# Gated recurrence and long convolution on one core: transposing before the sigmoid, the product in PSUM, and a new order

## The chip, the cores and the metric

The kernel runs on one core of a Trainium2 chip. The core has a matrix engine (TensorE, PE in the profile, with PEld for its weight loads), VectorE (DVE), ScalarE (ACT), GpSimd (POOL) and SyncE (SP), which here only issues transfers. Every engine takes its own queue of instructions strictly in order; between engines semaphores hold an instruction until its inputs are there. Data lie in SBUF or in PSUM, 128 partitions each; PSUM has eight banks of 512 float32 a partition, TensorE writes there only, and GpSimd can't reach it. The metric is the device time of one execution in microseconds. Before the change it was 462.54 us, the median of two runs (459.77 and 465.32).

## The reference

Four batches of 6,272 steps of 256 channels, float32 in and out. A gated recurrence runs along time, and a gated long convolution takes its result:

```python
sig = 1 / (1 + exp(-f_logit))
f = lower_bound + (1 - lower_bound) * sig
h[t] = f[t] * h[t-1] + (1 - f[t]) * x[t]
proj = h @ w_proj                      # 256 -> 768: x1, x2, x3
X2 = rfft(x2, n=S); H = rfft(filter_fft, n=S)
y = x1 * irfft(X2 * H, n=S) * x3
out = y @ w_out
```

With s = sigmoid(-f_logit), 1 - f = (1 - lower_bound) s. The factor (1 - lower_bound) belongs to a channel, so the kernel takes it out of the recurrence and puts it into w_proj. What is left is u = s x and f = 1 - (1 - lower_bound) s, and the scan h[t] = f[t] h[t-1] + u[t].

## The kernel before

The transform of length 6272 = 128 x 49 is made of matrix products. `prepare` makes its tables and the spectrum of the filter (lines 425 to 689) and stores the spectrum in DRAM as H. Then, for each batch:

- `hgrn` (312 to 371), the recurrence, in 13 chunks of 512 steps (the last has 128). SyncE loads a chunk of f_logit into FL and of x into XT (three buffers each), 512 KB a load, with time on the partitions. Step "sig": ScalarE makes s in place in FL. Step "u": GpSimd multiplies x by s in place in XT. Step "su": for each half kh of the channels, TensorE transposes s and u into two PSUM banks (16 transposes of each at a time), so that channels come onto the partitions. Step "f": ScalarE, or for some chunks VectorE, makes f out of s in PSUM and writes it to fTs in SBUF. Step "scan": VectorE scans f from SBUF and u from PSUM into HA; a chunk's scan starts from the last column of the chunk before. "wrap" copies the first 3,072 columns behind the end of HA.
- `spectrum`: `phase_p` (696 to 711, "P") makes x2 from all of HA, 13 groups of four residues of 49, each copied to SBUF (X2) by ScalarE or VectorE ("x2"). Then 16 units: F1 and its copy "A", the mini product for one frequency with VectorE's "zm" (738 to 745, two instructions), F2, the product with the spectrum (794 to 811), I2 and its copy "Th". The spectrum product has two forms: VectorE multiplies out of PSUM ("MUL", line 798), or ScalarE or VectorE copies to SBUF and GpSimd multiplies there (line 807).
- `gate` (374 to 419): x1 and x3 from HA, and their product z; here too VectorE multiplies out of PSUM (line 408), or two copies are made and GpSimd multiplies (line 417).
- `phase_o` (838 to 882): the last step of the inverse transform, VectorE's product with z ("y", line 857), the projection "proj", a copy and the store.

The recurrence of the next batch overwrites HA, so its scans run among the gate's and the inverse's work of this batch, behind P.

No scheduler decides while the program is built. `Plan` records the steps, each with the engines that may take it, and `ORDER` (lines 123 to 190) is a string that lists all steps in the order of issue: for each its engine and its PSUM bank. It is a constant in the source; `emit` follows it, and the costs that the steps carry are not read for it. So each queue's order, the choice of engine for every copy, f and product, and the banks come from that string. A step that takes PSUM names the number of banks (`take`), and the steps with `src` read what it left there.

Of the kernel before, what the change touches and what calls it, by code (L numbers as in the profile page):

```python
# [34 lines left out]
WARM = 24  # L35
# [4 lines left out]
FS = 1.0 / 8.0  # L40
HS = 64.0 / S / FS
# [4 lines left out]
NX2 = 13  # L46
# [13 lines left out]
class Plan:  # L60
# [63 lines left out]
    "A0gA1AA5gA6AA+gBDgBIgBNgBSgAAYAOYABIACIAPIApQAdQAzYAqQAoQAkQAyQARIA2QA/YA4AA3AAQAAVYAXYBXgAhSAlSBhgBAQBJYBCAAUIA"  # L124
    "WIAfSBBIA7SBEAAvUBcgBFUBOYBGEBHEAiWBKWBTYBLGBrgBMGBPUBREBYYAnWASABmgA9CA8KBwgBZWBiIBUQBdYBbOBVIBQEBjSBsYBlCBaGAT"
    "IBeUBgEBfEBnIBtWEFgAYYBuGBkCBWIBoUBxIAZYAaYBqEByQBzAB0AAxSD5gBpMB3SB4KD7AB5QB6IB7YBvOB+UD6gCASCBKB8QB/EB9AD8YCJU"
    "ADgAEYCKMCHSCDQCICCEICCYEHACQUCLYD9SERgETAEGgEBWD+KD/KEIYCREECGEDOCOQCPACMUCNEESgEUYCTQAFgCUAEJSEKKELKCXUCSYCYEE"
    "NQEdgB1YB2YEegEOAEVUAHAEfAEPIEgYEWMEXMEZWCeSCfCEpgEYYCZQCgSEaGEbOCaACcQCdICbYEqgCnUChCCiYE1gE2gEhSElWFBgCoMErAEs"
    "YAKAEiCFCgEjKEkYEmGEnOCpQCqACwUCrYAIACjQCxME3AE4YCkAEtSAJAEuKEvKExWFLgCuUGHgEyGEzOCvECyYCsQFMgFDAFEYE5UE6ME7ME9S"
    "CtAE+CFVgE/KEwYC5WE8YC6GCzQC0AC+WFNAFFUFIQFWgFfgFggFGMC2gC/GFJIDASC3WFOYDBCFHMC4GC7YDCYFXAFYYDHSC8WFKIFPUFQMFSQF"  # L130
    "pgFqgFRMC9GDICDDWDJSFTAFUIFZUFaMDEGDKCDLYFbMDOWFhAFiYFcQFzgF0gDPGFdAFeIDQSDRCDSYDZWDMUDTSFjQDNMCGgFrAFsYAGgDaGDU"
    "CFkIFlICmgDeWDfGDXUDYEDbYF1AF2YALADgSDhKFmWF9gF+gFnOFoODcUDdEFtQFuAFvIDpSCFgFwUDnWDqCDjSFxEFyMAMAE0YDiYEEYEcYEoY"
    "DoGDrYF/AGAYF3QF4IDkCFAYDuWDvOANAMegF5IDwUDxEC1gF6SF7CF8KEAYDsWEMYJbUJcVJeNMqgDyYJgQJhRGBSDtGClgJdECVgEQYJfYJiAG"
    "CKDzWJjBJkYGDKDWgGEUD3QGIgJlSJmTGFMGGMD0GD2gGtgJnKJorGJUGKED4ADVgGPWGQOGbSGcCGdUGeMGLQGMAGRSGSKGVUGWMMgAGXQGYIGZ"
    "SGaCDFgGTWGUOCWgMsAGNUGOMGhQGiIDGgGfSGgCJqWJrXD1gJvUJxMJwQJyoJzYJsGJtHJuYGjSGkCJ0RGpUGqEJ1QJ2BJ3IJ4YGuSGwqGxYGlW"
# [12 lines left out]
    "MASMBKMFWMGOOcUOdEOeMOfQVLgVKgOgAOhIMCSMDCMEgMHWM1YOmUOnEOpSOqCOoMOrKVWgMKQMLIMPUMQMMIGMJgO6SO7KO8WO9GPCQPDAO4UO"
    "5EO+SO/KPEQVAAVXgPFAVBYO0WO1GOuUOvEOyQOzIOwSOxKVMAVNYOsUOtMVYAO2QO3IPAWPBGMMSMNCMUUMVMPKQPLIVZYPGWPHGMRSMOgMSCMZ"
    "UMaMR/YSEYPQWPUuPVYPIQPJAPMUPNEMTgPSuPTYSFSSHKSGTSIDSJYMWQPOUPPMPZYPRYMXAPYWPogPauPbYPcuPdYPpSPrCPgUPkESKQSMAPWR"  # L150
    "PhYPlYPisPjYPXBPzVP0FP7gSLQSPXSRHSNoPeRPqYPtqPuYPsYSQUSUQSWIPfBPxWPyGSVVSXtSYYSSESTYP3SP4KP1QP2APmWP8UPnGQAsQBYP"
    "vQP5SP6KQGYP9YPwAP+sP/YQFWQHGQEgQIYQJuQKYSZVQNgSbFQfQQgAQXSQOVSaUQSFSeQSgAScsSdYQbKMYgQWgQCWQPYQTYQDGQQtQRYSfRSj"
    "QShpSiYSkTSlAQpgSmDQhWQiGQLUQYYQcYSnYQZqQaYQMEQjQQkAQUWQVGSOYQqUQygQusQvYSoSSqCQlQQmAQssQtYSpTQ7gQdWQeGSrrSsYStS"
    "SvCQnQQoIQrYQ0YQzUREgQ3EQ4YQ1sQ2YRFWRJGRHGRNSROKQwQQ9YQxAQ8UQ+ERAsRBYQ/YRXgVCWVDGRPQRQAVEOVGSVjgVigRggQ5URGYRIYR"
    "KYVHCVIKQ6ERpgVOQRCWVPAVQIRDGRRURSESuSSyTS0DSwqSxYRYWSzQRauRbYS1oS2YS3RS5BRcuRdYS4SRTUS8TS+LS6CS7YS9QVSRVvgVugRU"
    "ERVURWMRZYRygRLWRiYS/ATAYVTBVUJTBQRMGVkAVlYRhURjsRkYRlsRmYVaWVbGTDAReSRrYVcORfCTCRTGUTIETHQRqSRuqRvYTEBTFYVeUV7g"
    "V6gVmWTJATKYVFgVfEVgMRsCRtYVnGTLQTNATMRTQSTRTTOpTPYVoOVqUWHgWGgVwATSCTTrTUYVrEVsMRnQR0YVxYVJgRoATVSTWWTaXTXCTcHT"
    "bQTYuTZYRzSR1qR2YR3qR4YTdATeYV8ARwURxEVyQV2WWRgWQgVzAV0IV3GV4OTfSTgUTkTTiETlVTpUThCTqQTmDTntToYV9YTjYTrMWIAV+SV/"
    "CWCWWagTuRR5UTwBTvRWAKTzSTsoTtYTxpTyYWJYWDGWEOT0TT4QV1YR6EWbgT1CT2DT3YMbUT5RMcET6AT9SWKUWNWWSAWTYMdgT7pT8YWBAWkg"
    "WOGUCQWLEV5YWcAWdYWlgT+KT/SUACUBgUDIUEQUFAVdYWMMUHUWPOWUSWmAUIMUMWUGgWVCUNOWXQWWKWugWYAWZIWvgUJUUKEUOWUPGURSUSKW"  # L160
    "eUWhQWFYVVYWfEWgMULgVpAWiAW4gW5gabWUQgacXaeHWnYadGUTSUUCUVgUWUWwAWxYUbWWjIVhYUXMWoQWpAagSahTaiCajDUYUUZEUcOUgWWq"
    "IUhOWrSWyQXDgXCgWsCUdUWtKW1WWzAW0IW6AW7YW2GW3OUeEUagUiSUjCUlQUqUUmIUrMXEAXFYUfgdfgW8WW9GW+OW/SXACXBKdqgUnQUsUUoA"
    "UpgdegXGWXHGXJQd3gUkgXIOU0SVtYVRYXKAXLIU1KUtEUvWXiQXjAdrgUwOd2gXaUXbEXSSXTKXeQXfAXcUXdEXWSXXKdgAdsAXkQXlAdhYXOWX"
    "POUugdtYXYUXZEXMSXNKXgQXhAXUUXVMXQSXRCUxQUyAUzgU5UU6MafYXoSakYXmWXnOXpCXqUXrMXsQXtAalSanCamTaorU2WU3GU4gXuQXvIX5"
    "YXwUXyEX0sX1YXzYYIgdiSdjCX4QapYX8oX9YYTWYUGXxYX6oYbgaqUarVdkKasEavRatFaxBYAWYEGYCOauYdmUeCgdnEdoMX2QYBYX7YX3AYFY"
    "awXdlgayvYDYYkga0Sa2Ca1TX+QYKYa3ra4YYRUYSMazYd4Ad5YduWdySX/AeOga5QdvGdwOdzCd0KYVUa7AYWEa6Ra+Qa8BYJWYNuYOYYLuYMYb"
    "AAYXUYYEYGSYHCa/QbDRbBobCYa9Yd6UbFBYZSYaKYdYd7Ed8MYtgYcWYeGYfYYguYhYYPQYmYYQAYuSbEWYyCeDgYwCbGGYlQZBUZCEYnoYoYY2"
    "gbHYd+Seagd/CYpoYqYYiWYvYYjGeAKYxYZJgbIQbKAePgYzYbJUdpYbNVbLsbPFYrWY4YYsOZSgY/QeEAY3SY5qeFYY7qY8YZbgZFUZAAebgZGE"
    "Y6YbOWbSXbUHbQGbRYbTQbVoZDRY0UY1MY9WZEBZHQZIIZUYZLYd9YecAZKSZMqZOqZNYZtUZPYZTQZXoZYYY+GZuEZVoZWYbXWbZGZkgbYXbaHb"
    "bYbcSbeCbWYbdUeGWZcSbfEbgYeHGeIObMYZQUZdYZgqZhYZeCZfYedYZvRZREbhQZ3gZxUZwBbjAZZWZmYeQAZaObiRbkpblYbmQboAZlSZyEeJ"  # L170
    "gZnqZoYbnWZpqZqYZiQaAgbpGbqYZjAeRYZzUZ4WZ8uZ9YZ0EbrSZ6uZ7YaJgbsQbwRbtCaSgbuAbvYZrUeKSbyBZ1QZ2IaCYZ5YZsEeLCeMKemg"
# [22 lines left out]
def kernel(  # L194
# [230 lines left out]
    def prepare(head, tmp):  # L425
# [522 lines left out]
```

## Time and profile before

| | us |
|---|---|
| device time, median of 2 runs | 462.54 |
| the two runs | 459.77, 465.32 |
| span of the profiled execution | 460.2 |
| sigmoid on ScalarE, line 324, 52 instructions | 53.0 |
| product u on GpSimd, line 326, 52 | 116.9 |
| f on ScalarE, line 351, 89 | 58.3 |
| f on VectorE, line 353, 15 | 10.2 |
| scans on VectorE, line 359, 104 | 122.0 |

The profile is of one execution, and its span is the only time of that execution that is shown. A group of instructions is one source line, engine, operation and shape: busy time, mean of one in ns, and how long the engine stood idle before them and for whom. Instructions of one engine overlap at their ends, so the busy times of groups add up to a little more than the engine's. The ends of matrix products are modelled in the profile.

### The profile page before, as it was taken

The numbers are of one execution on the slowest core, as the hardware profiler recorded it, in microseconds if no ns is written. First come the engines' busy times: TensorE is split into PE (matmuls) and PEld (weight loads), VectorE is DVE, ScalarE is ACT, GpSimd is POOL, SyncE is SP. The second block draws the span as 40 slices with busy tenths as digits, with TensorE's granted clock in tenths as the row PEclk, the third lists the DMA queues.
The fourth block names the chain that finished last, engine by engine and source line by source line (L and its number), as shares of the span: only waits on it lengthen the run. The fifth ranks groups of instructions, "written<-read, shape, count | busy, mean of one in ns | idle before, by whom it ended". The sixth has DMA issues, their size and how long they took to land.

```text
span 460.2 us, 14622 instructions
## 1 busy us (share of the span) xinstructions
PE 439.7 (96%) x6009; PEld 344.3 (75%) x6009; DVE 412.1 (90%) x471; ACT 402.7 (88%) x582; POOL 310.2 (67%) x293
## 2 busy tenths in 40 slices
PE   7799989999989999999999999999999999999997
PEld 5677778766756889778667889767768897777786
DVE  8689998899999996998999996999999987999872
ACT  6799988799999997899999988999998868989663
POOL 6889766188999643778898435789996603857400
PEclk9899999999999999999999999999999999999999
DMA  8967898986997997386887996579869830756176
GB/s 333 390 268 288 315 307 283 349 284 219 309 353 250 358 315 276 139 246 218 307 300 280 318 317 239 214 248 318 255 235 315 306 138 13 230 200 205 57 287 275
DMA packets 44242, 121.40 MB, mean 264 GB/s; under 512 B 4240, under 2 KB 6672, under 8 KB 44176
## 3 DMA queue, kind: packets, MB, share of 16 engines
q1 hardware_dynamic: 44176, 120.47, 74.0%
q8 instruction: 47, 0.77, 0.7%
q14 instruction: 19, 0.16, 0.1%
HBM read 87.69 MB, written 31.98 MB: 260 GB/s over the span
## 4 chain that ended last, share of the span: by engine, by line
PE 63%; DVE 12%; ACT 11%; DMA 5%; issue 5%; POOL 2%; SPq 0%; DVEq 0%; ACTq 0%; POOLq 0%
PE PS L387 14%; PE PS L817 8%; PE PS L869 7%; PE PS L338 7%; PE PS L705 6%; PE PS L777 6%; PE PS L718 5%; DVE HA L359 5%; PE PS L851 4%; DMA FL<-in_f_logit_dram 3%; DVE ys L857 2%; DVE X L286 2%; ACT FL L324 2%; PE PS L646 2%; ACT fTs L351 1%
## 5 line engine op out<-in xcount | busy, mean ns | idle before, releaser
L326 POOL TENSOR_TENSOR XT<-XT,FL 128x1024 f32<-128x1024 f32 (+1 forms) x52 | 116.9, 2251 | 50.3 <-ACT FL L324 41.9
L359 DVE TENSOR_TENSOR_SCAN HA<-fTs,HA,PS 128x512 f16<-128x512 f32 (+1 forms) x96 | 112.5, 1200 | 2.8 <-ACT fTs L351 1.7
L798 DVE TENSOR_TENSOR PP<-PS,Hu 98x1008 f16<-98x1008 f32 x87 | 101.3, 1197 | 3.4 <-ACT HA L281 1.4
L387 PE MATMUL PS<-HA,W 128*128 128x490 f16 (+1 forms) x416 | 100.4, 367 | 0.9 <-DVE X L286 0.4
L807 POOL TENSOR_TENSOR PP<-HA,Hu 98x1008 f16<-98x1008 f16 x41 | 86.2, 2107 | 1.7 <-PE PS L817 1.0
L281 ACT CAST HA<-PS 128x1024 f16<-128x1024 f32 (+1 forms) x94 | 77.0, 849 | 5.1 <-PE PS L718 3.4
L417 POOL TENSOR_TENSOR zt<-x1s,x3s 128x490 f16<-128x490 f32 (+1 forms) x43 | 52.3, 1222 | 41.8 <-ACT x3s L281 22.9
L857 DVE TENSOR_TENSOR ys<-PS,zt 128x1024 fp32r<-128x1024 f32 (+1 forms) x52 | 58.5, 1149 | 9.5 <-PE PS L851 5.0
L283 ACT ACTIVATE osb<-PS 128x1024 f32<-128x1024 f32 (+1 forms) x51 | 49.9, 992 | 13.9 <-PE PS L869 11.2
L351 ACT ACTIVATE fTs<-PS,nomc 128x512 f32<-128x512 f32 (+1 forms) x89 | 58.3, 679 | 3.7 <-PE PS L338 2.3
L387 PEld LDWEIGHTS <-W 128*128 128x128 f16 x416 | 35.4, 97 | 31.7 <-issue 5.4
L869 PE MATMUL PS<-Wo,ys 128*128 128x256 f32 x392 | 57.7, 292 | 1.3 <-DVE ys L857 1.1
L283 ACT ACTIVATE x1s<-PS 128x490 f32<-128x490 f32 (+1 forms) x92 | 53.5, 594 | 5.0 <-PE PS L387 3.0
L817 PEld LDWEIGHTS <-PP 98*128 98x128 f16 x1024 | 48.7, 98 | 10.6 <-issue 3.1
L324 ACT ACTIVATE FL<-FL 128x1024 f32<-128x1024 f32 (+1 forms) x52 | 53.0, 1026 | 2.2 <-DMA FL<-in_f_logit_dram 2.1
L869 PEld LDWEIGHTS PS<-Wo,ys 128*128 128x128 f32 x392 | 49.4, 188 | 5.8 <-DVE ys L857 2.2
L817 PE MATMUL PS<-VA,PP 98*128 98x98 f16 x512 | 52.2, 207 | 1.5 <-ACT x1s L283 0.8
L817 PE MATMUL PS<-VB,PP 98*128 98x98 f16 x512 | 51.9, 207 | 0.0
L281 ACT CAST Th<-PS 128x784 f16<-128x784 f32 x58 | 48.2, 830 | 2.6 <-PE PS L817 1.6
L338 PE MATMUL PS<-iden,FL 64*128 64x64 f32 x784 | 44.8, 230 | 1.6 <-DVE HA L359 0.9
L705 PE MATMUL PS<-W,HA 128*128 128x256 f16 x392 | 44.4, 273 | 1.0 <-ACT X L281 1.0
L705 PEld LDWEIGHTS <-HA 128*128 128x128 f16 x392 | 42.9, 142 | 1.9 <-issue 1.3
(113 smaller groups left out, 724.3 us busy)
## 6 DMA issues: line engine op xcount, KB each, us to landing
Hu<-H SPq DMA_DIRECT2D x55, 512.0 KB, 4.4
FL<-in_f_logit_dram SPq DMA_DIRECT2D x48, 512.0 KB, 5.4
XT<-in_x_dram SPq DMA_DIRECT2D x48, 512.0 KB, 5.5
out_dram<-osb SPq DMA_DIRECT2D x48, 512.0 KB, 4.3
X<-in_moe_filter_fft_dram SPq DMA_DIRECT2D x9, 512.0 KB, 7.1
H<-Hu SPq DMA_DIRECT2D x4, 512.0 KB, 6.2
Hu<-in_moe_filter_fft_dram SPq DMA_DIRECT2D x2, 512.0 KB, 9.8
H<-Hu SPq DMA_DIRECT2D x4, 256.0 KB, 6.5
```

Source lines behind the costliest of these rows:

```text
L281: nc.scalar.copy(dst, src)
L283: nc.scalar.activation(dst, src, AF.Copy, scale=scale)
L326: op("u", {"POOL": 0.1 + 0.553 * nb}, lambda e, xt=xt, ft=ft: nc.gpsimd.tensor_tensor(xt, xt, ft, op=AOP.mult), r=[("ft", k)], w=[("xt", k)])
L338: nc.tensor.transpose(bank(pb)[:, at[p] + j:at[p] + hn:nb], src[ps, j, cols], iden[ps, ps])
L359: nc.vector.tensor_tensor_scan(h, fT, bank(pb)[:, 512 - hn:512 + hn], init, op0=AOP.mult, op1=AOP.add),
L387: nc.tensor.matmul(PS[:, p, 0:n], W13[:, kh, js], HA[:, HB[kh] + t0:HB[kh] + t0 + n], start=(kh == 0), stop=(kh == 1))
L705: nc.tensor.matmul(pp[:, r - r0, :], column(HB[kh], q_of(r)), W2[:, kh, :], start=(kh == 0), stop=(kh == 1))
L798: nc.vector.tensor_tensor(pr, px.unsqueeze(1).broadcast_to([TB, 2, UE, 63]), hh, op=AOP.mult)
L807: nc.gpsimd.tensor_tensor(pr, spec[:, o, :, 1:64].unsqueeze(1).broadcast_to([TB, 2, UE, 63]), hh, op=AOP.mult)
L817: nc.tensor.matmul(PS[:, ib + o, pr * TB:(pr + 1) * TB], PP[:TB, k, o, n, 2 * pr:2 * pr + 2, :], v[:TB], start=(n == 0), stop=(n == 1))
L857: nc.vector.tensor_tensor(late["ys"][:, yk, :, 0:rn * 128], PS[:, cb:cb + 2, 0:rn * 128], late["zt"][:].rearrange("p k r m -> p k (r m)") ...
L869: nc.tensor.matmul(po[:, i, :], late["ys"][:, yk, kh, i * 128:(i + 1) * 128], Wo[:, kh, :], start=(kh == 0), stop=(kh == 1))
```

## The change

In `hgrn`, the transposes move ahead of the arithmetic:

- f_logit and x are transposed as they were loaded, each with a step "su" of its own that takes two PSUM banks for both halves of the channels (before, one step for each half held s and u of that half). The number of transposes is the same.
- The sigmoid reads f_logit out of PSUM and writes s, now with channels on the partitions, back into FL.
- f is made from s in SBUF by ScalarE or GpSimd; fTs has one place for each half.
- u is made by VectorE, a product of x in PSUM and s in SBUF, written in place into the middle of the two PSUM banks, where the scan reads it. The second half's product writes where the first half's scan has read, so it waits for that.

Around it: P has 12 groups, the last of five residues over three banks; zm is one instruction of 256 elements in place of two of 128; the warming products come in 48 steps of two in place of 24 of four; and `ORDER` is a new string, so the choices of engine change too (counts over the whole run):

| step | before | after |
|---|---|---|
| f | ScalarE 89, VectorE 15 | ScalarE 32, GpSimd 72 |
| u | GpSimd 52 (of 1,024) | VectorE 104 (of 512) |
| spectrum product | VectorE 87, GpSimd 41 | VectorE 71, GpSimd 57 |
| its copies | ScalarE 39, VectorE 2 | ScalarE 52, VectorE 5 |
| gate product | VectorE 61, GpSimd 43 | VectorE 52, GpSimd 52 |
| gate copies | ScalarE 131, VectorE 16 | ScalarE 138, VectorE 18 |
| wrap | GpSimd 34, ScalarE 8, SyncE 6 | GpSimd 24, ScalarE 5, SyncE 19 |

```diff
+            fl = ft.rearrange("p j d -> p (j d)")
+            def turn(pb, src, at, nb=nb, hn=hn):
+                for kh in range(2):
+                    for j in range(nb):
+                        for p in range(2):
+                            ps, o = slice(64 * p, 64 * p + 64), at[kh][p]
+                            nc.tensor.transpose(bank(pb)[:, o + j:o + hn:nb],
+                                                src[ps, j, kh * 128:kh * 128 + 128], iden[ps, ps])
+            tz = op("su", ..., turn(pb, ft, ((0, 512), (256, 768))), r=[("ft", k), "iden"], take=2)
+            def gate_s(e, pb, fl=fl, hn=hn):
+                z = PS[:, pb:pb + 2].rearrange("p a (k t) -> p k a t", k=2)[:, :, :, 0:hn]
+                nc.scalar.activation(fl.rearrange("p (k a t) -> p k a t", k=2, a=2), z,
+                                     AF.Sigmoid, scale=-1.0)
-            op("sig", ..., nc.scalar.activation(ft, ft, AF.Sigmoid, scale=-1.0), w=[("ft", k)])
-            op("u", {"POOL": ...}, nc.gpsimd.tensor_tensor(xt, xt, ft, op=AOP.mult))
+            op("sig", ..., gate_s, w=[("ft", k)], src=tz)
+            tx = op("su", ..., turn(pb, xt, ((512 - hn, 512), (0, 768))), r=[("xt", k), "iden"], take=2)
             for kh in range(2):
-                su = op("su", ..., turn, r=[("ft", k), ("xt", k), "iden"], w=["qT"], take=2)
+                fT, sT = fTs[:, kh, 0:n], fl[:, kh * n:kh * n + n]
                 def gate_f(...):
                     if e == "ACT":
                         nc.scalar.activation(fT, sT, AF.Identity, scale=by, bias=1.0)
                     else:
-                        nc.vector.tensor_scalar(fT, in0=sT, scalar1=by, scalar2=1.0,
+                        nc.gpsimd.tensor_scalar(fT, in0=sT, scalar1=by, scalar2=1.0,
                                                 op0=AOP.mult, op1=AOP.add)
+                def gate_u(e, pb, sT=sT, kh=kh, hn=hn):
+                    mid = bank(pb)[:, 512 - hn:512 + hn]
+                    xT = halves(pb, hn) if kh else mid.rearrange("p (a t) -> p a t", a=2)
+                    nc.vector.tensor_tensor(mid.rearrange("p (a t) -> p a t", a=2), xT,
+                                            sT.rearrange("p (a t) -> p a t", a=2), op=AOP.mult)
+                op("u", {"DVE": ...}, gate_u, r=[("ft", k)] + ([("hn", 0, c)] if kh else []),
+                   w=[("uT", tx, kh)], src=tx)
...
-            for e2 in range(2):
-                nc.vector.tensor_tensor(zp[:TB, q % 2, e2], ..., Hm[:TB, e2, :, :, es], op=AOP.mult)
+            nc.vector.tensor_tensor(zp[:TB, q % 2], px, Hm[:TB, :, :, :, es], op=AOP.mult)
```

More of the change, by code (lines that the diff above doesn't have):

```diff
@@ L250 @@
     dram = ctx.enter_context(tc.tile_pool(name="dram", bufs=1, space=bass.MemoryType.DRAM))
[L252 removed]
+    H = [dram.tile([2, M + HT, 2 * UE * 64], F16, name=f"H{u}") for u in range(NU // 2)]
     psp = ctx.enter_context(tc.tile_pool(name="psp", bufs=1, space=PSUM))
@@ L323, in hgrn @@
                    w=[t], dma=0.38 * nb, lag=2.4, margin=MARGIN)
-            op("sig", {"ACT": 0.095 + 0.213 * nb}, lambda e, ft=ft: nc.scalar.activation(
-                ft, ft, AF.Sigmoid, scale=-1.0), w=[("ft", k)], table="sigmoid")
-            op("u", {"POOL": 0.1 + 0.553 * nb}, lambda e, xt=xt, ft=ft: nc.gpsimd.tensor_tensor(
-                xt, xt, ft, op=AOP.mult), r=[("ft", k)], w=[("xt", k)])
-            for kh in range(2):
-                cols = slice(kh * 128, kh * 128 + 128)
-                hn = 64 * nb
-                def turn(e, pb, ft=ft, xt=xt, cols=cols, nb=nb, hn=hn):
-                    for src, at in ((ft, (0, 768)), (xt, (512 - hn, 512))):
-                        for j in range(nb):
-                            for p in range(2):
-                                ps = slice(64 * p, 64 * p + 64)
-                                nc.tensor.transpose(bank(pb)[:, at[p] + j:at[p] + hn:nb],
-                                                    src[ps, j, cols], iden[ps, ps])
-                su = op("su", {"PE": 0.126 * nb}, turn, r=[("ft", k), ("xt", k), "iden"], w=["qT"], take=2)
-                j = count["f"] % 2
-                count["f"] += 1
-                fT = fTs[:, j, 0:n]
```

209 lines of the change are left out of this document (108 added, 101 removed).

## The prediction

> **What bounds the kernel now.** I read the page's head and its chain of waits first, then the chain in order of time to find where each batch's projection P begins (line 705), then the busy times between those points.
>
> ```profile
> span 460.2 us, 14622 instructions
> PE 439.7 (96%) x6009; PEld 344.3 (75%) x6009; DVE 412.1 (90%) x471; ACT 402.7 (88%) x582; POOL 310.2 (67%) x293
> PE 63%; DVE 12%; ACT 11%; DMA 5%; issue 5%; POOL 2%; SPq 0%; DVEq 0%; ACTq 0%; POOLq 0%
> ```
> ```profile
> 75.70 5.25 PE PS L705 x48
> ...
> 172.74 1.91 PE PS L705 x16
> ...
> 273.02 3.66 PE PS L705 x32
> ...
> 371.44 6.27 PE PS L705 x56
> ```
> ```profile
> 0.00:75.70 75.70, 66.60 (x707) 50.82 (x708) 66.77 (x103) 66.26 (x99) 61.81 (x86) 0.98 0.86 314
> 75.70:172.70 97.00, 92.52 (x1368) 71.62 (x1365) 90.33 (x98) 88.32 (x128) 69.11 (x55) 1.00 0.88 303
> 172.70:273.00 100.30, 98.43 (x1443) 77.56 (x1442) 93.56 (x99) 92.60 (x135) 72.06 (x59) 1.00 0.76 268
> 273.00:371.40 98.40, 96.99 (x1426) 76.57 (x1425) 91.27 (x97) 91.50 (x135) 72.92 (x59) 1.00 0.75 261
> 371.40:460.20 88.80, 85.15 (x1076) 67.71 (x1074) 70.19 (x78) 64.06 (x88) 34.33 (x35) 1.00 0.49 176
> ```
> ```profile
> 30.14:75.70 45.56, 42.47 (x550) 32.41 (x547) 44.22 (x48) 43.25 (x67) 38.69 (x42) 1.00 0.84 294
> ```
> ```profile
> 75.70:86.00 10.30, 10.30 (x97) 10.30 (x95) 8.51 (x9) 7.13 (x7) 0.92 (x1) 1.00 0.96 338
> ...
> sum 42.20, PE 41.16 PEld 40.58 DVE 29.31 ACT 31.19 POOL 8.65; mean PE 10.29 PEld 10.15 DVE 7.33 ACT 7.80 POOL 2.16
> ```
>
> The second line is the busy time of each engine in the span: the matrix engine (PE) and VectorE (DVE) are nearly full, ScalarE (ACT) a little less, GpSimd (POOL) a third idle. The chain puts 63% on PE, but PE has something queued almost always, so it appears in any chain; whether it waits for VectorE must be read from VectorE's own idle time. The third fence gives five stages, each from one P to the next: length, then busy time of PE, PE's weight loads, DVE, ACT and POOL, the granted clock (1.00), and DMA. The gate chain (lines 313 to 372) of a batch runs in the stage before its P. In the two full middle stages VectorE is idle for 6.7 and 7.1 us, and over half of that is P itself: the last fence takes the four P windows alone, where VectorE is busy 29.3 of 42.2 us, waiting for PE. In the first stage, from VectorE's first f at 30.14 on, it is busy 44.2 of 45.6 us. Outside P, VectorE is the engine with no room. Any net work put on it there is expected to lengthen the stage.
>
> **The prices.** The groups by shape, busy us and mean ns of one:
>
> ```profile
> L326 POOL TENSOR_TENSOR XT<-XT,FL 128x1024 f32<-128x1024 f32 x48 | 113.9, 2378 | 46.5 <-ACT FL L324 38.7 <-PE PS L387 4.5 <-DMA XT<-in_x_dram 2.4
> L326 POOL TENSOR_TENSOR XT<-XT,FL 128x256 f32<-128x256 f32 x4 | 2.9, 731 | 3.8 <-ACT FL L324 3.2 <-PE PS L338 0.6
> L351 ACT ACTIVATE fTs<-PS,nomc 128x512 f32<-128x512 f32 x83 | 56.2, 701 | 1.9 <-PE PS L338 1.3
> L353 DVE TENSOR_SCALAR fTs<-PS,nomc 128x512 f32<-128x512 f32 x13 | 9.5, 738 | 0.3 <-PE PS L338 0.3
> L324 ACT ACTIVATE FL<-FL 128x1024 f32<-128x1024 f32 x48 | 51.3, 1076 | 2.2 <-DMA FL<-in_f_logit_dram 2.1
> L281 ACT CAST HA<-PS 128x1024 f16<-128x1024 f32 x55 | 55.4, 1024 | 3.9 <-PE PS L718 3.4 <-POOL PP L807 0.2 <-issue 0.2
> L798 DVE TENSOR_TENSOR PP<-PS,Hu 98x1008 f16<-98x1008 f32 x87 | 101.3, 1197 | 3.4 <-ACT HA L281 1.4 <-DMA Hu<-H 1.0 <-PE PS L777 0.4
> L807 POOL TENSOR_TENSOR PP<-HA,Hu 98x1008 f16<-98x1008 f16 x41 | 86.2, 2107 | 1.7 <-PE PS L817 1.0 <-DVE zp L740 0.4 <-ACT HA L281 0.2
> L281 ACT CAST HA<-PS 98x512 f16<-98x512 f32 x39 | 22.0, 603 | 1.1 <-PE PS L777 0.9
> L408 DVE TENSOR_TENSOR zt<-PS,x1s 128x490 f16<-128x490 f32 x55 | 35.5, 656 | 1.6 <-ACT x1s L283 0.9 <-PE PS L387 0.2
> L408 DVE TENSOR_TENSOR zt<-PS,x1s 128x392 f16<-128x392 f32 x6 | 3.3, 559 | 1.0 <-PE PS L387 0.8 <-ACT x1s L283 0.2
> L417 POOL TENSOR_TENSOR zt<-x1s,x3s 128x490 f16<-128x490 f32 x41 | 50.2, 1231 | 40.1 <-ACT x3s L281 21.2 <-DVE ys L857 16.1 <-ACT x1s L283 1.9
> L740 DVE TENSOR_TENSOR zp<-PS,X 98x128 f16<-98x128 f32 x32 | 10.5, 371 | 1.5 <-PE PS L734 1.3
> L286 DVE CAST X<-PS 128x1024 f16<-128x1024 f32 x23 | 27.3, 1220 | 12.0 <-PE PS L705 9.7 <-ACT X L281 1.6 <-DMA H<-Hu 0.6
> L293 POOL COPY HA<-HA 128x512 f16<-128x512 f16 x34 | 20.1, 612 | 0.9 <-ACT W L470 0.8
> L581 POOL TENSOR_SCALAR ID<-PP,cols 128x256 f16<-128x256 f32 x2 | 1.8, 924 | 0.0
> L568 POOL TENSOR_SCALAR FT<-PP,cols 128x98 f16<-128x98 f32 x2 | 1.1, 566 | 0.0
> L630 POOL MEMSET X<- 128x1920 f16 x1 | 1.7, 1701 | 0.0
> L655 POOL CAST mX<-afs 128x16 fp32r<-128x16 f32 x16 | 3.2, 209 | 2.2 <-DVE afs L286 1.2 <-ACT afs L281 1.0
> ```
>
> Instructions on VectorE overlap at their ends, so a queue advances by less than their mean. The timeline of VectorE (start, length):
>
> ```profile
> 44.32 0.74 DVE L353 TENSOR_SCALAR fTs<-PS,nomc 128x512 f32<-128x512 f32 x1
> 45.10 2.45 DVE L359 TENSOR_TENSOR_SCAN HA<-fTs,HA,PS 128x512 f16<-128x512 f32 x2
> ...
> 341.29 1.85 DVE L408 TENSOR_TENSOR zt<-PS,x1s 128x490 f16<-128x490 f32 x3
> 343.06 0.42 DVE L288 TENSOR_SCALAR osb<-PS 128x256 f32<-128x256 f32 x1
> ...
> 345.50 2.44 DVE L359 TENSOR_TENSOR_SCAN HA<-fTs,HA,PS 128x512 f16<-128x512 f32 x2
> 347.85 2.33 DVE L857 TENSOR_TENSOR ys<-PS,zt 128x1024 fp32r<-128x1024 f32 x2
> ```
>
> Three L408 advance the queue by 343.06 - 341.29 = 1.77, 0.59 each against a mean of 0.656; two scans by 2.35. So I take 0.08 off every mean. A scan that reads what the instruction just before it wrote starts 0.04 after that one's end (45.10 against 45.06), where the independent successor at 347.85 starts 0.09 before the end (347.94): a dependent neighbour costs about 0.12.
>
> **The change, part by part, on VectorE.** Added: 104 products u, 96 of 512 and 8 of 128 elements. The nearest row is L408 (one operand in PSUM, one in SBUF, all float32): its slope is (656 - 559)/98 = 1.0 ns an element, so 0.61 for 512 and 0.23 for 128, in all 60.4. No row shows VectorE writing into PSUM, so this is bounded: slope alone, 0.51 (10 less), and L353's whole mean, 0.74 (12 more). Removed: 15 f, 13 at 0.66 and two short ones at about 0.26, 9.1. The new order also hands work away: direct spectrum products fall from 87 to 71 (16 x 1.12 = 17.9), direct gate products from 61 to 52 (9 x 0.58 = 5.2), VectorE's copies of 1,024 or so out of PSUM by nine, at 1.14, with small change (10.5), zm from 32 instructions of 128 to 16 of 256 (32 x 0.29 = 9.3 against 16 x 0.42 = 6.8). It gains five half-size copies, about 0.6 each (3.0). Net: 60.4 + 3.0 - 9.1 - 17.9 - 5.2 - 10.5 - 2.5 = +18 us.
>
> Then the new neighbours. In the order of the built kernel 52 scans stand directly behind the u that they read, and 34 u directly behind the scan whose operand they overwrite; before, some 13 such pairs. 73 x 0.12 = +9 us. Behind each such wait VectorE's next ys or spectrum product stands still, and PE waits for those. The Trainium skill (VectorE: DVE Perf Modes, "The DRAIN you can't avoid") says that a semaphore between chained VectorE instructions costs nothing extra. By that rule the sum is 9 us smaller; the two starts above speak against it here.
>
> **By stage**, since VectorE's order shows which stage each instruction is in. Before P(0): u +15.1, f -8.4, others -3.1, 21 pairs +2.5: +6. VectorE is full there from its first f to that P, so it shows. First middle stage: work -1.4, pairs +1.8; but VectorE copies three groups of P(0) instead of eight, and the next scans can't start before P ends, so up to five copies' time of the 8.51 busy us there falls idle and its other work follows later: between 0.4 and 6, I take +3. Second: +6.8 and 20 pairs: +9. Third: +5.6 and 18 pairs: +8. Last stage: +3.4, behind PE (85.2 busy of 88.8, VectorE 70.2): nothing. Of the idle time outside P, some 3 us may take up work. Together 6 + 3 + 9 + 8 - 3 = +23.
>
> **GpSimd** loses 52 u (113.9 + 2.9 = 116.8), and takes 72 of the 104 f, 16 spectrum products (33.7), 9 gate products (11.1), less ten wraps (6.1). What a 512 f costs no row shows. Lower end: the 512 copy, 0.61, 44 us in all. Upper end: TENSOR_SCALAR itself, (924 - 566)/158 = 2.3 ns an element, 1.5 us for 512, 108 in all. I take 1.5, the same operation. GpSimd then stands near 310 - 117 + 108 + 34 + 11 - 6 = 340, no bound over the run. Before P(0) it is one: 24 f are 36 us and its eight wraps, six gate products, fills and small copies from then on some 19, about 4.3 us for each of 13 chunks, against VectorE's 2 x (1.18 + 0.61) and 0.3 for pairs, 3.9. With the longer way from sigmoid to scan I put +4 on it. The Trainium skill (GPSIMD Engine Reference, "Engine selection") calls one-input work there roughly line-rate. By that the 4 us go; L581 speaks against it, at 924 ns for 256.
>
> **ScalarE** loses 57 f (about 0.6 each, 34) and gains 13 half copies (6.5) and several others (5): about -22. The sigmoid out of PSUM is nearer to 1024 (the cast of as many elements out of PSUM) than to 1076. None of this shortens a stage that VectorE ends. PE has the same transposes, products and inverse; P has 12 groups instead of 13. A f_logit buffer is now freed by the last u and f of its chunk, not by a transpose, so SyncE's loads queue behind VectorE; with three buffers and DMA at 0.86 before P(0) I give it nothing, and it would cost 2 or 3 us there. Thirteen more wraps go through SyncE, beside other transfers: nothing.
>
> Sum against the profiled execution: 460.2 + 23 + 4 = 487. Only its span is shown; the median of the two runs, 462.54, lies 2.3 above. I leave 487 for the device, since the bounds of u alone are wider.
>
> **The rivals.** (1) *Faster.* The chain no longer starts with a 2.4 us GpSimd product, transposes run as soon as a load lands, and PE, 63% of the chain, is fed earlier. For it: GpSimd waits 41.9 us for the sigmoid in all (38.7 + 3.2). Against it: VectorE must do 412 + 18 + 9 = 439; it decides where VectorE's idle time falls from 48 to under 14 (453 - 439), and the last stage has 18.6 of it, the P windows 12.9. Were 12 us of the last stage all that is left, the run would take 451. (2) *No change to be measured.* The pairs cost nothing and the 18 us fall half into idle time: 469. For it: VectorE and ScalarE together carry the same sum (+18 - 22). (3) *GpSimd's queue decides.* f stands behind two to four spectrum products of 2.1 us, and the scan behind f: where half of the 0.9 us extra for some 48 f in the middle stages shows, 487 + 21 = 508. (4) With u at its lower end and f at 0.61 the forecast's own mechanism gives 487 - 10 - 4 = 473.
>
> **How the numbers follow.** The forecast (with 4) 0.65, no change 0.18, GpSimd 0.11, faster 0.06. The range, 467 to 507, reaches just past the no-change case and up to GpSimd's; left out are the faster case, the lower part of no change and the upper half of GpSimd's, under 0.2 together. Measurements of this kernel tell apart about 2%: 453 to 472 is no change. Faster takes rival 1, 0.06; no change and a sliver of the forecast give 0.19; the rest is 0.75.
>
> **What would show it.** VectorE busy near 435 to 440, u at 0.65 to 0.72 mean, scans that start after the end of their u; the second and third middle stages some 8 us longer, the last unchanged; ScalarE near 380. A u under 0.6, an f on GpSimd of 0.65, or scans overlapping their u would take the steps away one by one. The forecast is wrong if VectorE's idle time outside P was not empty room lost but waiting that the new order removes.

## The result and the profile after

The changed kernel takes 496.19 us (median of 2 runs, 495.57 to 496.81), the kernel before 462.54 (459.77 to 465.32): 1.073 times as long, 95% interval 1.057 to 1.088. The profiled execution of the changed kernel has a span of 495.0 against 460.2, so 34.8 us to explain. The forecast was 487, between 467 and 507.

From the page of the changed kernel, the busy time of each engine, and the shares of the chain of waits that ended last:

```profile
PE 453.1 (92%) x6009; PEld 344.3 (70%) x6009; DVE 436.1 (88%) x512; ACT 393.1 (79%) x548; POOL 281.4 (57%) x330
...
PE 45%; DVE 17%; DMA 11%; ACT 10%; POOL 8%; issue 7%; DVEq 0%; ACTq 0%; POOLq 0%; SPq 0%
```

VectorE has 24.0 us more work (436.1 against 412.1), but its idle time rose too, from 48 to 59. PE's share of the chain fell from 63% to 45%, and what came in its place is not VectorE alone: transfers went from 5% to 11%, GpSimd from 2% to 8%. The busy time of PE rose without a single matmul more; the ends of its instructions are modelled, so the stages below are a better measure. They go from the first matmul of one P to the first of the next: the length, then the busy time of PE, PE's loads, VectorE, ScalarE, GpSimd, the granted clock, and DMA.

```profile
0.00:84.25 84.25, 71.85 (x749) 52.10 (x749) 72.82 (x111) 71.49 (x107) 52.49 (x99) 1.00 0.84 303
84.25:186.94 102.69, 93.18 (x1362) 72.53 (x1359) 91.44 (x103) 85.19 (x116) 60.00 (x62) 1.00 0.83 292
186.94:296.15 109.21, 102.76 (x1440) 77.80 (x1440) 100.49 (x114) 87.90 (x122) 65.89 (x67) 1.00 0.68 237
296.15:403.84 107.69, 100.29 (x1402) 75.77 (x1402) 98.51 (x109) 88.14 (x125) 65.67 (x66) 1.00 0.69 242
403.84:495.00 91.16, 84.98 (x1060) 66.07 (x1059) 72.83 (x78) 60.40 (x80) 37.35 (x37) 0.99 0.49 171
```

Against 75.5, 97.1, 100.3, 98.4 and 88.8 in the kernel before, the stages are 8.7, 5.6, 8.9, 9.3 and 2.3 longer. Four groups of instructions (busy time, mean ns of one, then the idle time of the engine ahead of them and what ended it):

```profile
L365 DVE TENSOR_TENSOR PS<-PS,FL 128x512 f32<-128x512 f32 (+1 forms) x104 | 68.6, 662 | 5.7 <-PE PS L334 2.6 <-ACT osb L285 1.2 <-issue 0.5
L357 POOL TENSOR_SCALAR fTs<-FL,nomc 128x512 f32<-128x512 f32 (+1 forms) x72 | 48.5, 676 | 101.4 <-DVE HA L371 48.7 <-ACT osb L285 15.3 <-DMA out_dram<-osb 12.7
L285 ACT ACTIVATE osb<-PS 128x1024 f32<-128x1024 f32 (+1 forms) x51 | 50.1, 988 | 34.1 <-DMA out_dram<-osb 15.1 <-PE PS L882 15.1 <-issue 1.6
L757 DVE TENSOR_TENSOR zp<-PS,X 98x256 f16<-98x256 f32 x16 | 9.5, 591 | 2.1 <-PE PS L749 1.5 <-ACT x3s L283 0.4
```

The product u (line 365) costs what was forecast. GpSimd's f (line 357) costs half of what was forecast, and GpSimd waits for the scans, not the scans for it. ScalarE's copies of the output stood 15.1 us behind stores, where the same group of the kernel before had 1.9:

```profile
L283 ACT ACTIVATE osb<-PS 128x1024 f32<-128x1024 f32 (+1 forms) x51 | 49.9, 992 | 13.9 <-PE PS L869 11.2 <-DMA out_dram<-osb 1.9 <-ACT x1s L283 0.4
```

The timeline of VectorE early in the changed kernel (start, length) shows the new neighbours, a u directly ahead of the scan that reads it:

```profile
33.29 0.70 DVE L365 TENSOR_TENSOR PS<-PS,FL 128x512 f32<-128x512 f32 x1 [0.23 <-PE PS L334]
34.10 1.28 DVE L371 TENSOR_TENSOR_SCAN HA<-fTs,HA,PS 128x512 f16<-128x512 f32 x1
35.41 0.70 DVE L365 TENSOR_TENSOR PS<-PS,FL 128x512 f32<-128x512 f32 x1
36.22 1.28 DVE L371 TENSOR_TENSOR_SCAN HA<-fTs,HA,PS 128x512 f16<-128x512 f32 x1
```

The scan starts 0.11 after the end of its u (34.10 against 33.99), the next u 0.03 after the end of that scan. An independent successor starts 0.08 before such an end, so these neighbours cost 0.19 and 0.11 on VectorE, where 0.12 was forecast. The Trainium skill (VectorE: DVE Perf Modes, "The DRAIN you can't avoid") reports of a row of copies that a semaphore behind each costs nothing extra; for these dependent pairs the starts above do not agree.

One piece of the chain of waits before P(0) was given nothing in the forecast's sum. Here it is in the changed kernel (start, length):

```profile
67.48 0.71 DVE PS L365
...
68.28 1.29 DVE HA L371
...
70.13 0.68 POOL fTs L357
...
70.85 4.82 DMA FL<-in_f_logit_dram
...
75.72 0.73 PE PS L334 x10
...
76.47 1.03 ACT FL L342
```

The load of f_logit starts when GpSimd has read the old contents of its buffer, and what stands behind it waits 4.8 us until it lands, 8.6 us before P(0). A load on the chain is not new in itself. The kernel before has one too, started when PE's transposes had read the buffer, but it lands some 15 us before its P(0):

```profile
54.39 0.48 PE PS L338 x8
...
54.92 5.97 DMA FL<-in_f_logit_dram
```

What is new is the pace. SyncE issues the f_logit loads of chunks 8 to 12 on average 4.9 us apart (51.08 to 70.85), in the kernel before 3.5 (44.41 to 58.22).

### The profile page after: what moved, and what is told of

It reads as the page before. It is cut to its first block, busy times and chain, and to the rows that moved or that the text cites. A ratio compares the mean times of both kernels' runs of the same rounds, so it can differ in the third digit from the quotient of the medians.

```text
span 495.0 us, 14864 instructions
## 1 busy us (share of the span) xinstructions
PE 453.1 (92%) x6009; PEld 344.3 (70%) x6009; DVE 436.1 (88%) x512; ACT 393.1 (79%) x548; POOL 281.4 (57%) x330
## 4 chain that ended last, share of the span: by engine, by line
PE 45%; DVE 17%; DMA 11%; ACT 10%; POOL 8%; issue 7%; DVEq 0%; ACTq 0%; POOLq 0%; SPq 0%
PE PS L398 10%; PE PS L721 9%; DVE HA L371 7%; DMA out_dram<-osb 7%; PE PS L334 5%; PE PS L830 5%; POOL PP L820 4%; PE PS L882 4%; DVE PS L365 4%; PE PS L790 4%; DMA Hu<-H 3%; PE PS L733 3%; ACT HA L283 3%; ACT osb L285 2%; DVE PP L811 2%
## 5 line engine op out<-in xcount | busy, mean ns | idle before, releaser
L820 POOL TENSOR_TENSOR PP<-HA,Hu 98x1008 f16<-98x1008 f16 x57 | 119.3, 2106 | 4.5 <-ACT HA L283 1.2
L371 DVE TENSOR_TENSOR_SCAN HA<-fTs,HA,PS 128x512 f16<-128x512 f32 (+1 forms) x96 | 115.4, 1207 | 4.6
L398 PE MATMUL PS<-HA,W 128*128 128x490 f16 (+1 forms) x416 | 107.8, 368 | 3.7 <-ACT FL L342 0.6
L357 POOL TENSOR_SCALAR fTs<-FL,nomc 128x512 f32<-128x512 f32 (+1 forms) x72 | 48.5, 676 | 101.4 <-DVE HA L371 48.7
L283 ACT CAST HA<-PS 128x1024 f16<-128x1024 f32 (+1 forms) x110 | 86.9, 815 | 12.1 <-PE PS L733 3.7
L428 POOL TENSOR_TENSOR zt<-x1s,x3s 128x490 f16<-128x490 f32 (+1 forms) x52 | 63.0, 1218 | 48.2 <-ACT x3s L283 27.2
L811 DVE TENSOR_TENSOR PP<-PS,Hu 98x1008 f16<-98x1008 f32 x71 | 83.3, 1198 | 3.6 <-PE PS L790 1.5
L285 ACT ACTIVATE osb<-PS 128x1024 f32<-128x1024 f32 (+1 forms) x51 | 50.1, 988 | 34.1 <-DMA out_dram<-osb 15.1
L365 DVE TENSOR_TENSOR PS<-PS,FL 128x512 f32<-128x512 f32 (+1 forms) x104 | 68.6, 662 | 5.7 <-PE PS L334 2.6
L342 ACT ACTIVATE FL<-PS 128x1024 f32<-128x1024 f32 (+1 forms) x52 | 50.8, 978 | 7.5 <-PE PS L334 7.0
L398 PEld LDWEIGHTS <-W 128*128 128x128 f16 x416 | 33.9, 97 | 31.2 <-issue 12.3
L283 ACT CAST X<-PS 128x1024 f16<-128x1024 f32 (+1 forms) x27 | 27.9, 1085 | 17.0 <-PE PS L721 15.8
```

The source lines that it names most:

```text
L283: nc.scalar.copy(dst, src)
L285: nc.scalar.activation(dst, src, AF.Copy, scale=scale)
L365: nc.vector.tensor_tensor(mid.rearrange("p (a t) -> p a t", a=2), xT, sT.rearrange("p (a t) -> p a t", a=2), op=AOP.mult)
L371: lambda e, pb, h=h, fT=fT, hn=hn, init=init: nc.vector.tensor_tensor_scan(h, fT, bank(pb)[:, 512 - hn:512 + hn], init, op0=AOP.mult, op1= ...
L398: nc.tensor.matmul(PS[:, p, 0:n], W13[:, kh, js], HA[:, HB[kh] + t0:HB[kh] + t0 + n], start=(kh == 0), stop=(kh == 1))
L428: nc.gpsimd.tensor_tensor(zd(), xs(0), xs(1), op=AOP.mult)
```

## The experiments

The theories in the order in which they came up. 1: VectorE is the bound, and its net new work is the loss. 2: the dependent neighbours on VectorE are a loss of their own. 3: the new order, and transfers on the SP queue, are the loss. 4: GpSimd's f is late. Later ones: 5, each order is fitted to the work it was made for; 6, VectorE and ScalarE's copies are two limits close together; 7, ScalarE's copies alone are the limit.

Times are medians of 4 runs each, beside 7 runs of the kernel before on the same chip (461.9 to 463.4 in the four sets). The changed kernel itself was timed only at first, with 2 runs, so differences from it are between sets and carry that spread, some 1.5 us.

**Without the product.**

```diff
-                    nc.vector.tensor_tensor(mid.rearrange("p (a t) -> p a t", a=2), xT,
-                                            sT.rearrange("p (a t) -> p a t", a=2), op=AOP.mult)
+                    pass
```

> Leaves the product of x and s out (VectorE scans the turned x itself); the order, the queues, GpSimd's f, the loads and the stores are as in the changed kernel. Theory 1 (VectorE is the bound, and the net work that the product puts on it is the loss): VectorE's busy time falls from 436 to about 370 us, and the time by 25 to 45 us, to 450 to 470, where another engine takes over. Theory 3 (the new order, and transfers that stand on the SP queue behind loads that wait for VectorE, are the loss): the time stays above 485, though 66 us of VectorE's work are gone.

Measured: 491.51 (489.25 to 493.43), 1.063 times the kernel before (1.058 to 1.068). All of the product is gone from VectorE, and 4.7 us from the time. The page and the two full middle stages of this run:

```profile
PE 451.6 (92%) x6009; PEld 343.9 (70%) x6009; DVE 376.2 (77%) x408; ACT 391.7 (80%) x548; POOL 281.2 (57%) x330
```

```profile
184.46:292.27 107.81, 102.09 (x1443) 77.74 (x1441) 86.12 (x87) 87.80 (x123) 65.24 (x67) 1.00 0.69 246
292.27:397.80 105.53, 99.18 (x1404) 75.58 (x1403) 83.69 (x82) 86.80 (x125) 65.55 (x66) 1.00 0.68 243
```

VectorE is busy 86.1 of 107.8 us and 83.7 of 105.5, about 22 us idle in each stage, and the stages are still 7 us longer than before. Theory 1, as it stood, falls: in this order something else holds the time almost as high as VectorE does. That the order (theory 3) is all of the loss does not follow either: with VectorE's work gone, one cannot see what stands next.

**A short product.** Every instruction and wait stays; 8 of 512 columns are computed.

```diff
-                    nc.vector.tensor_tensor(mid.rearrange("p (a t) -> p a t", a=2), xT,
-                                            sT.rearrange("p (a t) -> p a t", a=2), op=AOP.mult)
+                    nc.vector.tensor_tensor(mid[:, 0:8], xT[:, 0, 0:8], sT[:, 0:8], op=AOP.mult)
```

> Computes the product for 8 of its 512 columns: every instruction and every wait of the product stays, and nearly all of its work goes. Theory 2 (an instruction that needs the result of the one just before it on VectorE costs some 0.1 to 0.2 us beside its work, 13.6 us over the 86 such pairs, part of it already in the step from u to scan): above the run without the product by 10 to 25 us. If the work alone is the loss: above it by less than 8 us.

Measured: 491.98 (491.26 to 492.92), 0.5 above the run without it. Its group:

```profile
L365 DVE TENSOR_TENSOR PS<-PS,FL 128x8 f32<-128x8 f32 x104 | 17.7, 171 | 15.7 <-PE PS L334 8.0 <-ACT x1s L285 3.8 <-ACT FL L342 1.0
```

The 104 instructions bring back 17.7 us of work and all waits for nearly nothing. But VectorE has some 18 us to spare in a full middle stage here, so this says little on what a wait costs where VectorE is full.

**Neighbours moved apart.** Only the table of the order changes: 16 products one place ahead on VectorE, so that another instruction stands between them and their scan.

```diff
 ORDER = (
-...
+...
 )
```

> Moves 16 of the products one place ahead on VectorE, so that a product stands directly ahead of its own scan 36 times and not 52 (and directly behind the scan that it waits for 38 times and not 34). Theory 2: 16 x 0.19 less 4 x 0.11 us, about 3 us faster (a third of that is still lost where VectorE has idle time). Theories 1 and 3: no change within 1.5 us.

Measured: 505.80 (503.83 to 508.39), 9.6 slower where 3 faster was expected. The groups show why it could not gain:

```profile
L365 DVE TENSOR_TENSOR PS<-PS,FL 128x512 f32<-128x512 f32 (+1 forms) x104 | 68.8, 665 | 11.0 <-PE PS L334 5.7 <-ACT x1s L285 1.7 <-issue 1.5
```

A product moved ahead waits for its transposes (5.7 us of idle time, 2.6 in the changed kernel), and what stood ahead of it now stands behind it. The measured 0.19 and 0.11 a pair remain true on VectorE; that they are a loss in the time was not shown. Of the 9.6 us, 5.5 lie before P(0) (89.8 against 84.3), and what they are was not followed. What the run does show is how much 16 places in an order can cost.

**A short f on GpSimd.**

```diff
-                def gate_f(e, fT=fT, sT=sT, kh=kh):
+                def gate_f(e, fT=fT, sT=sT, kh=kh, m=n if b == 0 and c == 0 else 8):
...
-                        nc.gpsimd.tensor_scalar(fT, in0=sT, scalar1=by, scalar2=1.0,
+                        nc.gpsimd.tensor_scalar(fT[:, 0:m], in0=sT[:, 0:m], scalar1=by, scalar2=1.0,
```

> GpSimd computes 8 of the 512 columns of every f that it has but those of the first chunk (the others keep old values). Theory 4 (f on GpSimd is late, its latency or its queue sets when a scan starts): faster by 8 us or more. Theory 1: no more than 3 us, GpSimd has 213 us to spare.

Measured: 498.25 (497.25 to 499.31), no gain. The group fell from 48.5 to 20.3 us:

```profile
L357 POOL TENSOR_SCALAR fTs<-FL,nomc 128x8 f32<-128x8 f32 (+1 forms) x72 | 20.3, 283 | 111.0 <-DVE HA L371 47.8 <-ACT osb L285 14.9 <-ACT FL L342 13.5
```

Theory 4 is out for the changed kernel: f's work on GpSimd is off the path there, and no scan is seen to wait for it. In the run without the product that changes: there the scans waited 8.7 us for GpSimd's f, in 12 places.

**Stores issued by ScalarE**, in the changed kernel, in the kernel before, and in the one without the product. The edit is the same in all three:

```diff
-            op("store", {"SP": 0.46}, lambda e, k=k, r0=r0, rn=rn: nc.sync.dma_start(
+            op("store", {"SP": 0.46}, lambda e, k=k, r0=r0, rn=rn: nc.scalar.dma_start(
```

> The 52 stores of the output are issued by ScalarE, right behind the copy into their buffer, and no longer by SyncE, where they stand behind loads that wait for buffers; nothing else is changed. The product x times s on VectorE stays. Theory 3 (transfers that stand behind others on the SP queue are the loss): the 35 us that the chain of waits has on stores (7% of 495) go for a good part, and ScalarE's idle time ahead of the output copies falls from 34 to about 15 us: faster by 10 to 25 us, 470 to 486. Theory 1 (VectorE's work): no gain, and up to 5 us slower for 52 more instructions on ScalarE.

> The same edit in the kernel before. Theory 3: the kernel before does not lose time there (its ScalarE idles 1.9 us for stores), so no change within 4 us. If it gains as much as the changed kernel does, the queue is no part of the difference between the two.

> Both: the product is left out (VectorE scans the turned x itself), and the stores are issued by ScalarE. If the two losses only cover each other: below the sum of both single gains, 450 to 468. If the order itself, apart from the stores, is the loss: 475 or more.

Measured: 504.99 (503.61 to 505.31), 472.06 (470.76 to 475.50) and 493.85 (492.33 to 494.78): 8.8, 9.2 and 2.3 slower than without the edit. Theory 3's numbers were missed (470 to 486, and no change within 4), and theory 1's 5 us at most as well. With both edits the time is above 475, as was expected if the order, apart from the stores, is the loss. ScalarE's group of output copies, in the changed kernel with the edit and in the one without the product with it:

```profile
L285 ACT ACTIVATE osb<-PS 128x1024 f32<-128x1024 f32 (+1 forms) x51 | 50.3, 989 | 35.9 <-PE PS L882 15.0 <-DMA out_dram<-osb 14.6 <-PE PS L864 2.2
```

```profile
L285 ACT ACTIVATE osb<-PS 128x1024 f32<-128x1024 f32 (+1 forms) x51 | 50.1, 988 | 36.1 <-DMA out_dram<-osb 18.6 <-PE PS L881 13.6 <-DVE ys L869 1.5
```

The wait for stores stays at 14.6 and 18.6 us, though each store is now issued right behind its copy. So it was not the place on the SP queue, and as an explanation of the loss the queue falls. What is left is that the copies come closer together, so that three buffers do not last for stores that take some 4.4 us from issue to landing (4.3 before): a copy starts a median 6.5 to 7.3 us after the third one ahead of it in the three first batches, in the kernel before 7.9 to 8.7. A fourth buffer, which would test this, was not tried.

**Another order, by the same search, for three kernels**: the changed one, the one without the product, and the one before. Each operation stays on its engine; its place in the queues and its PSUM banks change, by a search over the queues played with durations from the traces. Only the table of the order differs.

```diff
 ORDER = (
-...
+...
 )
```

> The changed kernel with every operation on the engine that it had, in another order on the engines' queues and with other PSUM banks, found by a search that plays the queues with durations and waits read from the traces of both kernels. Theory 3 (the new order is the loss, not the new work): with a better order it comes close to the kernel before, 475 or less. Theory 5 (each order is fitted to the work it was made for, and the product costs its time in any order): the search has about 10 us to gain, as it has in the kernel before: 482 to 490.

> The same search for the changed kernel without the product (VectorE scans the turned x itself). Theory 5: the run without the product gained 5 us only because all other queues kept an order that was made around it; with an order made without it, 15 to 25 us below the reordered kernel that has the product: 462 to 472. Theory 3: the product costs no more than the 5 us seen, so within 8 us of the reordered kernel that has it.

> The same search for the kernel before, as a measure of what a search gains where nothing was changed. Theory 5: about as much as in the changed kernel, 10 to 13 us, 449 to 453, so that the distance of the two kernels stays 25 us or more. Theory 3: the kernel before has a good order already, it gains less than 4 us.

Measured: 504.85 (503.53 to 506.12), 482.94 (480.60 to 484.60) and 475.95 (475.57 to 476.62). As an attempt to find better orders it failed: the changed kernel and the one before lost 8.7 and about 13 us. Its use is the comparison under one hand. Two orders made in the same way, with and without the product, are 21.9 us apart, not 4.7; and the two whole kernels are 28.9 apart where the originals are 33.7. Theory 5 expected 15 to 25 between the first two and 25 or more between the two whole kernels, which came, but also that the search would gain some 10 us in each whole kernel and bring the one without the product to 462 to 472, which did not. Theory 3's numbers (the changed kernel at 475 or less, the product within 8 us) were missed. Of the 22.6 us between the two spans, 503.6 and 481.0, 10.3 lie before P(0) (93.2 against 82.9), and the reordered kernel lost there what it lost in all (93.2 against 84.25); so the 21.9 is no clean price of the product. Behind P(0) the two are 12.3 apart.

**ScalarE's copies cut, with the product and without it.** With the product in place and without, ScalarE copies only a few columns of A, Th and the output; the rest keeps old values. The core of the edit, the same form three times:

```diff
-        op("A", either(1024), lambda e, pb: copy(
-            e, A[:, k:k + UE],
-            PS[:, pb:pb + 2].rearrange("p a (i r k) -> p (a i) r k", r=2, k=64)),
+        def a_out(e, pb):
+            i, c = (1, 8) if e == "ACT" and b else (UE, 64)
+            copy(e, A[:, k:k + i, :, 0:c],
+                 PS[:, pb:pb + 2].rearrange("p a (i r k) -> p (a i) r k", r=2, k=64)[:, 0:i, :, 0:c])
+        op("A", either(1024), a_out,
...
```

> The changed kernel with its product, and with ScalarE's copies out of PSUM cut short: of A and Th (from the second sequence on) and of the output (from the fourth store on) it copies a few columns, some 100 us of its 393 us of work less; order, waits, loads and stores stay. Theory 6 (VectorE is the limit, and ScalarE's copies are a second limit right behind it, which is why the product alone could be left out for 5 us): VectorE holds the time, 488 to 497. Theory 7 (ScalarE's copies are the limit, and the product on VectorE never was): 484 or less.

> Both: the product left out (VectorE scans the turned x itself), and the same copies of ScalarE cut short. Theory 6: with both limits gone the time falls by more than the sum of the two single gains, to 465 to 480. Theory 3 (the order of the queues and the transfers are the loss): no more than the sum of the single gains, 483 or more.

Measured: 493.44 (492.75 to 494.60) and 481.17 (480.50 to 484.19). Together with the first two this is a square:

| us | ScalarE's copies whole | cut |
|---|---|---|
| product in place | 496.2 | 493.4 |
| product left out | 491.5 | 481.2 |

Leaving out the product is worth 4.7 with whole copies and 12.3 with cut ones; cutting the copies is worth 2.8 with the product and 10.3 without. Both together give 15.0, twice the sum of the single gains. That is how two limits of nearly the same height behave: taking one down shows the other. Theory 7 is out, as 94 us less of ScalarE's work changed the time by 2.8. Theory 6 fits the square, and its 488 to 497 with the product came, but its 465 to 480 without it was missed by 1 us: 481.2 is still 18.7 above the kernel before. The page of the last run, and its two full middle stages:

```profile
PE 448.7 (94%) x6009; PEld 343.7 (72%) x6009; DVE 375.6 (78%) x408; ACT 298.7 (62%) x548; POOL 280.4 (59%) x330
```

```profile
180.91:286.83 105.92, 100.74 (x1443) 76.85 (x1441) 86.01 (x87) 58.94 (x125) 65.26 (x67) 1.00 0.71 252
286.83:389.03 102.20, 97.91 (x1405) 75.13 (x1404) 83.64 (x82) 57.98 (x123) 65.40 (x66) 1.00 0.71 251
```

No engine but PE is near full there, and the stages are still 5.6 and 3.8 us longer than in the kernel before, which had more work on VectorE, ScalarE and GpSimd. The lengths of the stages in the profiled executions, from P to P:

| us | to P(0) | first | second | third | last |
|---|---|---|---|---|---|
| before | 75.5 | 97.1 | 100.3 | 98.4 | 88.8 |
| changed | 84.3 | 102.7 | 109.2 | 107.7 | 91.2 |
| product left out | 83.6 | 100.8 | 107.8 | 105.5 | 91.8 |
| ScalarE's copies cut | 84.8 | 100.9 | 108.7 | 107.0 | 89.6 |
| both | 82.8 | 98.1 | 105.9 | 102.2 | 89.7 |
| product left out, reordered | 82.9 | 98.3 | 105.8 | 101.7 | 92.4 |

With both, the first middle stage and the last stage come back to within 1 us of the kernel before; the stretch before P(0) hardly moves in any run of the square. The last row is the reordered kernel without the product, with ScalarE's copies whole: but for the last stage it is as fast as "both", and it took 482.9. So another place in the queues does for the run without the product what cutting the copies does. The square shows that VectorE's work was hidden behind a second limit; whether that is ScalarE's copies as work or the order in which they stand, it doesn't tell.

## Why the prediction was right, and where it was not

The direction, the range and the most likely case came out: slower by 34 against the 24 forecast. That the time came so near is in part luck, as the steps show:

**VectorE's work.** Held: busy 436.1 where 435 to 440 was forecast, u at 662 ns mean over both sizes (0.65 to 0.72). The 104 u are 68.6 us busy; less the overlap of 0.08 each that the sum takes off, that is 60.3, where 60.4 was put. One zm takes 591 ns where about 0.5 was put. VectorE's work rose by 24.0, not 18: 73 more dependent pairs lose 0.08 of overlap each, 5.8 by estimate, and so a part of the forecast's 9 for the pairs shows as busy time.

**The neighbours.** Held on VectorE in kind, and somewhat larger: 52 x 0.19 + 34 x 0.11 = 13.6 for all 86 pairs, where 0.12 each would be 10.3 (the forecast's 9 is less the 13 pairs of before). That they lengthen the run was never shown: moving 16 of them cost 9.6, for reasons that were not followed.

**GpSimd.** Wrong in its price, and the 4 us on it should not be in the sum. The row of 256 elements at 924 ns was taken; f took 698 for 512, and cutting it short changed nothing. The rule of the Trainium skill beside it (GPSIMD Engine Reference, "Engine selection": one-input work roughly line-rate) was the better guide, and the trace agrees with it: 698 and 272 ns for 512 and 8 columns are 0.8 ns an element, and VectorE's f of the same size, out of PSUM, took 738 in the kernel before.

**"Outside P, VectorE is the engine with no room. Any net work put on it there is expected to lengthen the stage."** This is the step that failed as it was put. Had VectorE alone been the limit, leaving out 60 us of its work would have brought back most of the loss; it brought 4.7. In its place the runs show limits close together: VectorE, just behind it a second one that goes when ScalarE's copies are cut or the order is changed, and something further at about 481 that no run names. The sum came out near the result because the new order held other queues at about the height of VectorE's, which the prediction had not said; it did not name all that was lost.

**By stage.** Forecast 10, 3, 9, 8, 0, less 3 in all; measured 8.7, 5.6, 8.9, 9.3, 2.3. The shape is right. The 3 of the first middle stage had its reason right, VectorE idle while P(0) runs, and 5.6 lies within its bounds of 0.4 to 6. VectorE stands idle there for 5.5 us at once:

```profile
84.34 0.48 DVE L371 TENSOR_TENSOR_SCAN HA<-fTs,HA,PS 128x128 f16<-128x128 f32 x1
90.34 1.22 DVE L288 CAST X<-PS 128x1024 f16<-128x1024 f32 x1 [5.52 <-PE PS L721]
```

In the second and third stages VectorE's books agree as well, with 6.9 and 7.2 us more work and 2.0 more idle time in each; yet without the product they stay 7.5 and 7.1 longer than before, so the agreement doesn't show the cause. The reason for the first number is wrong: VectorE's +6 and GpSimd's +4 were to make it, but without the product the stretch still takes 83.6, with VectorE busy 56.7 of it. That 10 came near 8.7 is luck. Given nothing, with "2 or 3 us there" in case, was the buffer of f_logit, which is now free only after the last f and u. The chain above points to it: 4.8 us of load on the path just before P(0), and loads that follow each other every 4.9 us and not 3.5. In the run without the product the same load stands there with 7.1:

```profile
67.50 0.58 ACT x3s L283
...
68.11 7.11 DMA FL<-in_f_logit_dram
...
75.26 0.73 PE PS L334 x12
```

In both it lands at about 75.5 us, whatever VectorE does, and without the product the loads still come 4.4 us apart (50.38 to 68.11). That these loads are the 8.7 us is not shown: the kernel before has one on its chain as well, and an experiment (a fourth buffer, or the loads left out) was not made.

**SyncE's queue and the stores.** Given nothing. The wait of ScalarE for stores rose from 1.9 to 15.1 us, but not by the queue; that the copies come closer together is the likely cause, and was not tested. What it cost is not settled.

**The rivals.** GpSimd's queue (508) is excluded in the changed kernel by the short f and by its scans, none of which is seen to wait for GpSimd. No change (469) and faster (451) counted on VectorE's idle time being used; it rose from 48 to 59 us instead.

What stays open: with the product out and ScalarE's copies cut, 18.7 us are left. By the spans 7.3 of them lie before P(0), where the load above stands on the chain, and 9.4 in the second and third stages (105.9 and 102.2 against 100.3 and 98.4). The order on PE and its PSUM banks, 16 more spectrum products on the longer way over ScalarE and GpSimd, and the stores are candidates that no run told apart. So the cause of the 34 us is shown only in part.

## What to carry to other kernels

An engine that is busy nine tenths of a stage is not shown to be its limit: an order that was made around it lets the other queues rise to the same height, and then no single cut gains much. Test two suspects alone and together; a gain of both that is larger than the sum of the two is the sign of limits close together, though it doesn't say whether the second one is work or order. Where a buffer's last reader moves down the pipeline, look at the pace of the loads that refill it, not only at the work that was moved.

## What the runs showed of the hardware

Issuing a DMA from ScalarE held up its work. In the kernel before, with its stores issued by ScalarE (timeline of ScalarE: start, length, idle time):

```profile
161.35 1.02 ACT L283 ACTIVATE osb<-PS 128x1024 f32<-128x1024 f32 x1 [0.49 <-PE PS L851]
162.41 0.34 ACTq L879 DMA_DIRECT2D out_dram<-osb  x1
162.79 1.27 ACT L351 ACTIVATE fTs<-PS,nomc 128x512 f32<-128x512 f32 x2 [0.42 <-ACT osb L283]
```

The issue starts 0.04 after the end of the copy whose result it stores, takes 0.34, and the next instruction starts 0.04 after that: 0.42 us in which ScalarE does nothing. With 52 of them the two whole kernels were 9 us slower, and the one without the product 2.3.

A product of 8 columns in PSUM took 171 ns and one of 512 took 693, so about 0.16 us of each is fixed and 1.04 ns an element comes on top; and VectorE multiplied PSUM by SBUF back into the same PSUM banks at about the pace at which it wrote to SBUF (656 ns for 490 elements before). The scan behind a product in PSUM started 0.11 us after the product's end, where behind an f in SBUF it had started 0.04 after; what makes the difference no run separates.
